# Steps 16 to 44 of a fused attention and gated feed-forward kernel: maxima and exponentials at the scheduler's highest rank

## The chip, the cores and the metric

The kernel runs on one core of a Trainium2 chip. The metric is the device time of one execution in microseconds; the runs of the kernel before took 446.5 us in the median of three (445.61 to 447.54). TensorE (PE) multiplies matrices, VectorE (DVE), ScalarE (ACT) and GpSimd (POOL) do the rest, SyncE (SP) issues most loads. Each engine works through its own row of instructions in order, and waits on semaphores where it needs another engine's result.

## What is computed

Attention with a local window and a few global keys, then a feed-forward layer with a short convolution as its gate. Cut to what matters:

```python
scores = scale * q @ k.T + bias        # bias: -slope[h] * distance
scores = where(is_global | is_local, scores, -1e9)
a = exp(scores - max(scores)); a = a / (sum(a) + 1e-9)
x = heads_joined(a @ v)                # 4 x 768 x 512
h = relu(x @ w_in)                     # 512 -> 1024
conv = conv3_over_positions(h, conv_w)
out = (h * sigmoid(conv)) @ w_out      # 1024 -> 512
```

There are 4 batches, 8 heads of width 64, 768 positions, a window of 96 keys and 8 global keys.

## The kernel before

The work is cut into 32 **jobs**: a batch, a half of its positions (384) and a pair of heads. A job has three **steps** of 128 query rows, so there are 96 steps, numbered through. Four jobs (12 steps) make one half of a batch, after which the feed-forward layer of that half can run.

One step runs through five stages. `scores` (lines 376 to 404) multiplies queries with the 232 keys in reach for both heads into a PSUM tile `s` (two buffers; up to job 8 the second head's half stands in a tile `sb` of its own). `maxima` (line 412) adds the table of distances and takes the row's minimum of the negated scores on DVE. `exps` (line 426) takes the exponentials on ACT and writes them to one of three buffers `pbuf`; where a job starts a new batch it also clears a few columns on GpSimd (line 424). `normalise` (lines 437 to 444) takes the reciprocal of the sums on DVE and scales the rows on GpSimd (and, up to step 31, on ACT). `transposes` (line 452, PE) and `evict` (line 457, ACT) bring the rows into the form `pt` that `values` (line 473, PE) multiplies with `v` into `pv`. `pv` has one PSUM bank; it is free for the next job when `mixed_high` (line 485, ACT) and `mixed_low` (line 489, DVE) have split it into `xh` and `xl`. In a name like `s41`, `mm39`, `pt38` the number is the step; in `pv12`, `xl11`, `kk14` it is the job.

The feed-forward layer uses the same splits: `h` (line 507) is the first product in three parts (`xh` with the high weights, `xl` with them, `xh` with the low weights), lines 555 to 559 are the convolution into `c`, line 577 its hyperbolic tangent, line 610 the gating, lines 612 and 613 the split into `gh` and `gl`, line 622 the second product `o`. Lines 316 to 331 decode the weights from their 64-bit words; lines 137 to 142 split queries and keys into `qh`, `ql` and `kk`.

Steps 0 to 15 are written in an order by hand. From step 16 on, the loop only states the work, and a scheduler lays out each engine's row when the kernel is built: of what its own reckoning holds ready, it takes first what has the higher rank, and rank falls in the order in which the program states the work. `values` already states its work at the highest rank. `tc.issue_after` puts some pieces behind a step's last maximum or exponential. No row can change while the kernel runs.

Of the kernel before, what the change touches and what calls it, by code (L numbers as in the profile page):

```python
# [34 lines left out]
LAG_T, LAG_V = 2, 4  # L35
NPB = 3
SHARED = 32
CHECK_EVERY = 3
HAND = 16
NATIVE = 9  # L40
# [27 lines left out]
def fast_path(tc, io):  # L68
# [273 lines left out]
    def check_piece(k):  # L342
        x = words[k]
        junk = p2.tile([P, HW], F32, tag="qh", name=f"junk{k}")
        j2 = p2.tile([P, HW], F32, tag="ql", name=f"junkb{k}")
        V.tensor_tensor_reduce(
            out=junk, in0=x, in1=x, scale=-1.0, scalar=-3.0e38,
            op0=ALU.mult, op1=ALU.max, accum_out=chk[:, k : k + 1],
        )
        A.activation(j2, x, AF.Square, accum_out=chk[:, NCHK + k : NCHK + k + 1])  # L350
        if len(words) < NCHK:
            check_load()
# [51 lines left out]
    def maxima(s):  # L404
        m, i = steps[s]
        b, u, hp = jobs[m]
        sp, c0, n, first = st_s[s]
        mm = p1.tile([P, 8], F32, tag="mm", name=f"mm{s}", bufs=6)
        for j in range(2):
            h = 2 * hp + j  # L410
            tb = tab[:, h, WIN:] if first else tab[:, h, 0:WIN]
            last_ttr[s] = V.tensor_tensor_reduce(  # L412
                out=sp[j][:, c0 : c0 + n], in0=sp[j][:, c0 : c0 + n], in1=tb,
                scale=-0.125, scalar=3.0e38, op0=ALU.add, op1=ALU.min,
                accum_out=mm[:, j : j + 1],
            )
        st_s[s] = (sp, c0, n, mm)

    def exps(s):
        m, i = steps[s]  # L420
        sp, c0, n, mm = st_s[s]
        pb = pbuf[s % NPB]
        if c0 and s and steps[s][0] % (2 * NPAIR) == 0:
            G.memset(pb[:, :, 0:c0], 0.0)
        for j in range(2):
            last_exp[s] = A.activation(  # L426
                pb[:, j, c0 : c0 + n], sp[j][:, c0 : c0 + n], AF.Exp,
                bias=mm[:, j : j + 1], scale=-1.0, accum_out=mm[:, 2 + j : 3 + j],
            )
        st_s[s] = (pb, c0, n, mm)  # L430
        if s < SHARED:
            A.activation(mm[:, 4:6], mm[:, 2:4], AF.Identity, bias=eps)

    def normalise(s):
        pb, c0, n, mm = st_s[s]
        if s >= SHARED:
            V.tensor_scalar(mm[:, 4:6], mm[:, 2:4], 1.0e-9, None, ALU.add)
        V.reciprocal(mm[:, 6:8], mm[:, 4:6])  # L438
        for j in range(2):
            x, inv = pb[:, j, c0 : c0 + n], mm[:, 6 + j : 7 + j]  # L440
            if j and s < SHARED:
                A.activation(x, x, AF.Copy, scale=inv)  # L442
# [268 lines left out]
    def check_some(cost):  # L711
        pace[0] += cost
        while pace[1] < NCHK and pace[0] >= CHECK_EVERY * (pace[1] + 1):
            check_piece(pace[1])
# [70 lines left out]
    for s in range(len(steps) + LAG_V + 1):  # L785
# [36 lines left out]
        else:  # L822
# [3 lines left out]
                manual.__exit__(None, None, None)  # L826
            if s < len(steps):
                scores(s)
                maxima(s)
                exps(s)  # L830
            k = 0
            e = s - LAG_V - 1
            if e >= 0:
# [181 lines left out]
def build(nc, io):  # L1015
    with tile.TileContext(nc, schedule_with_timeline_sim=True) as tc:
        fast_path(tc, io)
# [49 lines left out]
```

## Time and profile before

| | before |
|---|---|
| median of three runs | 446.5 us (445.61 to 447.54) |
| the profiled execution | 445.31 us |
| its span | 443.5 us |
| granted clock of PE, mean | 0.996 |
| PE busy | 431.2 us, 97% |
| DVE busy | 357.2 us, 81% |
| ACT busy | 309.9 us, 70% |
| POOL busy | 221.2 us, 50% |

The span runs from the first instruction to the last, and 1.8 us lie around it. Busy times overlap, so they don't add up. Matmuls are pipelined: one of 512 columns shows some 400 ns, while the next starts after about 234 ns, so PE counts as busy where one follows the other without a gap. A row's own work is therefore taken from start to start.

### The profile page before, as it was taken

How to read it: one execution, taken by the hardware profiler on the slowest of the kernel's cores; microseconds unless marked ns; L12 is line 12 of the kernel's file. 1: busy time of each engine (PE TensorE's matmuls, PEld its weight loads, DVE VectorE, ACT ScalarE, POOL GpSimd, SP SyncE). 2: the span in 40 equal slices, each digit the busy share in tenths (PEclk: the TensorE clock that was granted, in tenths of full speed). 3: DMA queues.
4: the chain of work that ended last, by engine and by line, in shares of the span. 5: the costliest groups of instructions: out<-in, count | busy, mean ns of one | idle time of the engine just before them, and what ended most of it. 6: DMA issues, size and time to landing. Idle time of an engine off the chain costs nothing.

```text
span 443.5 us, 9050 instructions
## 1 busy us (share of the span) xinstructions
PE 431.2 (97%) x3039; PEld 374.5 (84%) x3039; DVE 357.2 (81%) x935; ACT 309.9 (70%) x839; POOL 221.2 (50%) x307
## 2 busy tenths in 40 slices
PE   8988999799999999999999999999999999999996
PEld 7655778799889988899889988899988998798876
DVE  6899899998999988757998989747999975568700
ACT  4889988789896678546876865665776776755540
POOL 5555334654456786556757744647656841013000
PEclk9999999899999999999999999999999999999999
DMA  6998953141543244442246134423235313980111
GB/s 210 294 255 258 271 184 110 40 163 65 153 128 120 75 136 132 128 125 94 85 128 192 41 107 145 141 102 104 67 119 181 103 48 122 312 295 32 47 49 55
DMA packets 22662, 60.02 MB, mean 135 GB/s; under 512 B 3024, under 2 KB 5584, under 8 KB 22608
## 3 DMA queue, kind: packets, MB, share of 16 engines
q1 hardware_dynamic: 18992, 53.01, 39.2%
q10 hardware_dynamic: 3616, 6.36, 3.9%
q8 instruction: 26, 0.43, 0.4%
q14 instruction: 28, 0.23, 0.2%
HBM read 53.07 MB, written 6.29 MB: 134 GB/s over the span
## 4 chain that ended last, share of the span: by engine, by line
PE 81%; DVE 8%; DMA 6%; ACT 3%; issue 1%; POOL 0%; SPq 0%; DVEq 0%; ACTq 0%
PE o L622 26%; PE h L507 25%; PE pv L473 10%; PE t L452 9%; PE s L395 7%; DMA check<-in_w 3%; PE s L385 1%; PE last L643 1%; DMA out<-ob 1%; DVE w L320 1%; DVE w L318 1%; ACT junkb L350 1%; ACT pbuf L426 1%; DMA rq<-in_qk 1%; PE sb L385 1%
## 5 line engine op out<-in xcount | busy, mean ns | idle before, releaser
L444 POOL TENSOR_SCALAR pbuf<-pbuf,mm 128x232 f32<-128x232 f32 (+1 forms) x160 | 113.3, 718 | 81.0 <-DVE mm L438 49.5
L426 ACT ACTIVATE pbuf<-s,mm 128x232 f32<-128x232 f32 (+1 forms) x165 | 72.1, 442 | 48.3 <-DVE mm L412 34.6
L412 DVE CUSTOM_DVE_ANT_0 s<-s,tab 128x232 f32<-128x232 f32 (+1 forms) x165 | 63.1, 385 | 20.2 <-PE s L395 15.7
L622 PE MATMUL o<-woh,gh 128*128 128x512 f32 x184 | 74.1, 403 | 0.0
L622 PE MATMUL o<-woh,gl 128*128 128x512 f32 x184 | 73.5, 400 | 0.0
L622 PE MATMUL o<-wol,gh 128*128 128x512 f32 x184 | 73.3, 398 | 0.0
L452 PE MATMUL t<-ident,pbuf 128*128 128x128 f32 x384 | 65.4, 279 | 5.4 <-ACT pbuf L442 2.7
L557 POOL TENSOR_SCALAR c<-hbuf,cw 128x382 f32<-128x382 f32 (+1 forms) x48 | 38.6, 807 | 56.5 <-ACT hbuf L517 56.5
L452 PEld LDWEIGHTS t<-ident,pbuf 128*128 128x128 f32 x384 | 46.4, 141 | 20.2 <-ACT pbuf L442 6.4
L457 ACT ACTIVATE pt<-t 128x512 f32<-128x512 f32 x96 | 57.0, 597 | 8.3 <-PE t L452 8.0
L507 PE MATMUL h<-xl,wih 128*128 128x384 f32 x252 | 59.4, 343 | 0.0
L507 PE MATMUL h<-xh,wih 128*128 128x384 f32 x252 | 58.8, 347 | 0.1
L507 PE MATMUL h<-xh,wil 128*128 128x384 f32 x252 | 55.8, 339 | 0.0
L473 PE MATMUL pv<-pt,v 128*64 128x128 f32 (+1 forms) x768 | 50.3, 280 | 0.3 <-DVE xl L489 0.2
L473 PEld LDWEIGHTS pv<-pt,v 128*64 128x64 f32 (+1 forms) x768 | 42.5, 138 | 8.6 <-issue 3.6
L558 DVE SCALAR_TENSOR_TENSOR c<-hbuf,cw,c 128x382 f32<-128x382 f32 (+1 forms) x64 | 44.3, 699 | 4.8 <-POOL c L557 3.7
L559 DVE SCALAR_TENSOR_TENSOR c<-hbuf,cw,c 128x382 f32<-128x382 f32 (+1 forms) x64 | 45.4, 712 | 0.3
L507 PEld LDWEIGHTS h<-xh,wih 128*128 128x128 f32 x252 | 43.2, 190 | 2.1 <-ACT pbuf L426 0.9
L507 PEld LDWEIGHTS h<-xl,wih 128*128 128x128 f32 x252 | 43.9, 189 | 0.7 <-issue 0.7
L507 PEld LDWEIGHTS h<-xh,wil 128*128 128x128 f32 x252 | 44.1, 188 | 0.0
L517 ACT ACTIVATE hbuf<-h 128x384 f32<-128x384 f32 x64 | 31.4, 495 | 13.5 <-PE h L507 12.5
L622 PEld LDWEIGHTS o<-woh,gl 128*128 128x128 f32 x184 | 34.6, 188 | 7.3
(120 smaller groups left out, 856.1 us busy)
## 6 DMA issues: line engine op xcount, KB each, us to landing
v<-in_vv SPq DMA_DIRECT2D x32, 384.0 KB, 3.6
rq<-in_qk SPq DMA_DIRECT2D x23, 384.0 KB, 3.1
wr<-in_w SPq DMA_DIRECT2D x16, 512.0 KB, 5.3
check<-in_w SPq DMA_DIRECT2D x16, 512.0 KB, 4.9
rk<-in_qk SPq DMA_DIRECT2D x12, 504.0 KB, 3.6
out<-ob ACTq DMA_DIRECT2D x23, 256.0 KB, 2.4
rk<-in_qk SPq DMA_DIRECT2D x11, 408.0 KB, 3.6
rq<-in_qk SPq DMA_DIRECT2D x16, 96.0 KB, 5.1
```

The costliest lines, as they stand in the source:

```text
L412: last_ttr[s] = V.tensor_tensor_reduce(out=sp[j][:, c0 : c0 + n], in0=sp[j][:, c0 : c0 + n], in1=tb, scale=-0.125, scalar=3.0e38, op0=ALU. ...
L426: last_exp[s] = A.activation(pb[:, j, c0 : c0 + n], sp[j][:, c0 : c0 + n], AF.Exp, bias=mm[:, j : j + 1], scale=-1.0, accum_out=mm[:, 2 + ...
L444: G.tensor_scalar(x, x, inv, 1.0, ALU.mult, ALU.mult)
L452: T.transpose(pt[:, j, c, :], pb[:, j, c * P : (c + 1) * P], ident)
L457: last_ev[s] = A.activation(sb, st_pt[s], AF.Copy)
L473: T.matmul(pv[m][64 * j : 64 * j + 64, i * P : (i + 1) * P], vt[m][:n, i, c, 64 * j : 64 * j + 64], sb[:n, j, c, :], start=c == 0, stop=c ...
L507: T.matmul(ps[:, :TB], w_[:, k, fs], x_, start=part == 0 and k == 0, stop=part == 2 and k == NK - 1,)
L517: A.activation(half, ps[:, :TB], AF.Relu, scale=0.5)
L557: G.tensor_scalar(c, *tap(1), 1.0, ALU.mult, ALU.mult)
L558: V.scalar_tensor_tensor(c, *tap(0), c, ALU.mult, ALU.add)
L559: V.scalar_tensor_tensor(c, *tap(2), c, ALU.mult, ALU.add)
L622: last = T.matmul(ps, g_[:, f], w_[:, f], start=f == 0 and part == 0, stop=f == NF - 1 and part == 2,)
```

## The change

In the part that the scheduler lays out, `maxima` and `exps` of steps 16 to 44 are stated at the highest rank; a constant `FIRST` holds the first step that isn't. That covers, for each step, two maxima on DVE with their two read-outs, two exponentials on ACT, up to step 31 one addition to the sums on ACT, and twice the clearing of columns on GpSimd. The instructions stay the same; only their order in the rows, and with it the order of all that the scheduler lays out around them, differs, from 61.5 us on in the trace of before to some 236 us.

```diff
--- before.py
+++ after.py
@@ -35,6 +35,7 @@
 LAG_T, LAG_V = 2, 4
 NPB = 3
 SHARED = 32
+FIRST = 45
 CHECK_EVERY = 3
 HAND = 16
 NATIVE = 9
@@ -826,8 +827,11 @@
                 manual.__exit__(None, None, None)
             if s < len(steps):
                 scores(s)
-                maxima(s)
-                exps(s)
+                with contextlib.ExitStack() as es:
+                    if s < FIRST:
+                        es.enter_context(tc.high_priority())
+                    maxima(s)
+                    exps(s)
             k = 0
             e = s - LAG_V - 1
             if e >= 0:
```

What that does to the rows is shown at three places. The numbers behind the underscore are the build's own; lines of the changed kernel are one higher than before.

PE, at the scores of step 22 (`s22` one head, `sb22` the other), before:

```order
L385 MATMUL s22_1070<-rk7_794,rq7_795 128x232
L473 MATMUL pv5_1026<-pt17_957,v5_800 64x128 x4
L473 MATMUL pv5_1026<-pt15_854,v5_800 64x128 x4
L473 MATMUL pv5_1026<-pt16_915,v5_800 64x128 x4
L452 MATMUL t19_1042<-ident_153,pbuf1_194 128x128 x2
L385 MATMUL sb22_1071<-rk7_794,rq7_795 128x232
```

and with the change:

```order
L386 MATMUL s22_1070<-rk7_794,rq7_795 128x232
L386 MATMUL sb22_1071<-rk7_794,rq7_795 128x232
L474 MATMUL pv5_1026<-pt17_957,v5_800 64x128 x4
L474 MATMUL pv5_1026<-pt15_854,v5_800 64x128 x4
L474 MATMUL pv5_1026<-pt16_915,v5_800 64x128 x4
L453 MATMUL t19_1042<-ident_153,pbuf1_194 128x128 x4
```

The second head's scores moved ahead of the values of job 5.

DVE, up to the split `xl6` of job 6, before:

```order
L141 TENSOR_TENSOR kk10_1335<-rk10_1253,kk10_1335 64x816
L320 SCALAR_TENSOR_TENSOR w7_0_1250<-wr7_0_1010,w7_0_1250 128x512
L558 SCALAR_TENSOR_TENSOR c0_865<-hbuf_190,cw_185,c0_865 128x382
L412 ISA s27_1285,mm27_1290<-s27_1285,tab_166 128x136
L412 ISA mm27_1290 128x1
L438 RECIPROCAL mm26_1261<-mm26_1261 128x2
L316 TENSOR_SCALAR w7_1_1329<-wr7_1_1065 128x512
L331 TENSOR_TENSOR wol_189<-w6_1_1199,woh_188 128x512
L412 ISA s28_1342,mm28_1347<-s28_1342,tab_166 128x232
L412 ISA mm28_1347 128x1
L489 TENSOR_TENSOR xl6_1222<-pv6_1171,xh6_1221 128x384
```

and with the change:

```order
L317 TENSOR_SCALAR w7_1_1329<-wr7_1_1065 128x512
L332 TENSOR_TENSOR wol_189<-w6_1_1199,woh_188 128x512
L413 ISA s28_1342,mm28_1347<-s28_1342,tab_166 128x232
L413 ISA mm28_1347 128x1
L319 SCALAR_TENSOR_TENSOR w7_1_1329<-wr7_1_1065,w7_1_1329 128x512
L559 SCALAR_TENSOR_TENSOR c0_865<-hbuf_190,cw_185,c0_865 128x382
L142 TENSOR_TENSOR kk10_1335<-rk10_1253,kk10_1335 64x816
L413 ISA s28_1342,mm28_1347<-s28_1342,tab_166 128x232
L413 ISA mm28_1347 128x1
L490 TENSOR_TENSOR xl6_1222<-pv6_1171,xh6_1221 128x384
L439 RECIPROCAL mm26_1261<-mm26_1261 128x2
```

The second maximum of step 27 stands next to the first, `kk10` went behind it, and `w7_1` of line 318 (319 now) and the second maximum of step 28 came ahead of `xl6`.

PE, at the values of job 7, which need `xl6` done, before:

```order
L452 MATMUL t24_1270<-ident_153,pbuf0_193 128x128 x4
L395 MATMUL s29_1399<-kk9_1204,qh9_1202 128x232
L395 MATMUL s29_1399<-kk9_1204,ql9_1203 128x232
L395 MATMUL s29_1399<-kk9_1204,qh9_1202 128x232
L395 MATMUL s29_1399<-kk9_1204,ql9_1203 128x232
L473 MATMUL pv7_1299<-pt23_1233,v7_1068 64x128 x4
L473 MATMUL pv7_1299<-pt21_1133,v7_1068 64x128 x4
L473 MATMUL pv7_1299<-pt22_1192,v7_1068 64x128 x4
```

and with the change:

```order
L453 MATMUL t24_1270<-ident_153,pbuf0_193 128x128 x4
L474 MATMUL pv7_1299<-pt23_1233,v7_1068 64x128 x4
L474 MATMUL pv7_1299<-pt21_1133,v7_1068 64x128 x4
L474 MATMUL pv7_1299<-pt22_1192,v7_1068 64x128 x4
L396 MATMUL s29_1399<-kk9_1204,qh9_1202 128x232
L396 MATMUL s29_1399<-kk9_1204,ql9_1203 128x232
L396 MATMUL s29_1399<-kk9_1204,qh9_1202 128x232
L396 MATMUL s29_1399<-kk9_1204,ql9_1203 128x232
```

The scores of step 29 went from ahead of the values to behind them.

DVE, at the split `xl11` of job 11, before:

```order
L412 ISA s39_1903,mm39_1908<-s39_1903,tab_166 128x232
L412 ISA mm39_1908 128x1
L489 TENSOR_TENSOR xl11_1974<-pv11_1917,xh11_1973 128x384
L613 TENSOR_TENSOR gl0_2_1577<-hbuf_190,gh0_2_1576 128x8x2
L438 RECIPROCAL mm38_1874<-mm38_1874 128x2
L141 TENSOR_TENSOR kk14_1956<-rk14_1865,kk14_1956 64x1008
L412 ISA s39_1903,mm39_1908<-s39_1903,tab_166 128x232
L412 ISA mm39_1908 128x1
L610 SCALAR_TENSOR_TENSOR hbuf_190<-c1_1541,hbuf_190 128x8x128
L613 TENSOR_TENSOR gl0_3_1851<-hbuf_190,gh0_3_1850 128x1024
L412 ISA s40_1963,mm40_1968<-s40_1963,tab_166 128x232
L412 ISA mm40_1968 128x1
```

and with the change (the rows further up are `gl0_2`, `gl0_3`, a maximum of step 39, a gating and `gl0_4`, which before stood behind `xl11`):

```order
L614 TENSOR_TENSOR gl0_4_1947<-hbuf_190,gh0_4_1946 128x1024
L142 TENSOR_TENSOR kk14_1956<-rk14_1865,kk14_1956 64x1008
L438 TENSOR_SCALAR mm39_1908<-mm39_1908 128x2
L413 ISA s40_1963,mm40_1968<-s40_1963,tab_166 128x232
L413 ISA mm40_1968 128x1
L614 TENSOR_TENSOR gl0_5_2001<-hbuf_190,gh0_5_2000 128x1024
L413 ISA s41_2018,mm41_2023<-s41_2018,tab_166 128x232
L413 ISA mm41_2023 128x1
L490 TENSOR_TENSOR xl11_1974<-pv11_1917,xh11_1973 128x384
L439 RECIPROCAL mm39_1908<-mm39_1908 128x2
L413 ISA s40_1963,mm40_1968<-s40_1963,tab_166 128x232
L413 ISA mm40_1968 128x1
```

`xl11` moved behind eleven instructions that followed it before.

PE, at the values of job 12, which need `xl11` done, before:

```order
L507 MATMUL h2_2_2062<-xl11_1974,wih_186 128x384
L507 MATMUL h2_2_2062<-xh8_1521,wil_187 128x384
L507 MATMUL h2_2_2062<-xh9_1677,wil_187 128x384
L507 MATMUL h2_2_2062<-xh10_1832,wil_187 128x384
L507 MATMUL h2_2_2062<-xh11_1973,wil_187 128x384
L473 MATMUL pv12_2094<-pt38_1992,v12_1820 64x128 x4
L473 MATMUL pv12_2094<-pt36_1894,v12_1820 64x128 x4
L473 MATMUL pv12_2094<-pt37_1938,v12_1820 64x128 x4
L395 MATMUL s42_2067<-kk14_1956,qh14_1954 128x232
```

and with the change:

```order
L508 MATMUL h2_2_2062<-xh11_1973,wih_186 128x384
L508 MATMUL h2_2_2062<-xl8_1522,wih_186 128x384
L508 MATMUL h2_2_2062<-xl9_1678,wih_186 128x384
L508 MATMUL h2_2_2062<-xl10_1833,wih_186 128x384
L474 MATMUL pv12_2094<-pt38_1992,v12_1820 64x128 x4
L474 MATMUL pv12_2094<-pt36_1894,v12_1820 64x128 x4
L474 MATMUL pv12_2094<-pt37_1938,v12_1820 64x128 x4
L508 MATMUL h2_0_2005<-xl11_1974,wih_186 128x384
L508 MATMUL h2_0_2005<-xh8_1521,wil_187 128x384
L508 MATMUL h2_0_2005<-xh9_1677,wil_187 128x384
L508 MATMUL h2_0_2005<-xh10_1832,wil_187 128x384
```

The third part of `h2_0`, `h2_1` and `h2_2` (with `wil`) and their product with `xl11`, 15 matmuls, moved from ahead of the values to behind them.

## Rows read from the trace of the kernel before

**Rows 1.** The page, part 1: engine, busy us (share of the span), weight loads and others behind it.

```profile
PE 431.2 (97%) x3039; PEld 374.5 (84%) x3039; DVE 357.2 (81%) x935; ACT 309.9 (70%) x839; POOL 221.2 (50%) x307
```

**Rows 2.** Busy time by stage: stretch, its us, busy us of each engine, PEclk, DMA share, GB/s.

```profile
80.00:120.00 40.00, 37.70 (x287) 34.84 (x287) 38.03 (x91) 34.03 (x92) 19.05 (x23) 0.96 0.35 108
...
120.00:160.00 40.00, 40.00 (x288) 36.21 (x287) 39.01 (x92) 30.95 (x81) 27.63 (x31) 1.00 0.33 101
```

**Rows 3.** PE in order of time: start, us, line, form, count [idle before, released by].

```profile
39.41 0.44 PE L452 MATMUL t<-ident,pbuf 128*128 128x128 f32 x2 [1.04 <-DMA rq<-in_qk]
...
81.49 0.60 PE L452 MATMUL t<-ident,pbuf 128*128 128x128 f32 x4
...
84.15 0.38 PE L395 MATMUL s<-kk,qh 128*128 128x232 f32 x1 [2.06 <-ACT pbuf L426]
...
85.10 2.61 PE L473 MATMUL pv<-pt,v 128*64 128x128 f32 x24 [0.24 <-DVE xl L489]
...
87.64 1.11 PE L452 MATMUL t<-ident,pbuf 128*128 128x128 f32 x4
...
92.20 1.54 PE L473 MATMUL pv<-pt,v 128*64 128x128 f32 x24
```

**Rows 4.** Busy time by stage, with the granted clock, around three places of rows 3.

```profile
39.40:41.40 2.00, 1.99 (x24) 1.53 (x26) 1.97 (x8) 1.80 (x7) 1.38 (x2) 1.00 0.72 194
...
84.00:86.00 2.00, 1.61 (x15) 1.43 (x16) 2.00 (x5) 2.00 (x8) 1.36 (x2) 0.84 0.04 15
...
86.00:88.00 2.00, 2.00 (x19) 1.67 (x17) 2.00 (x6) 0.70 (x2) 0.00 (x0) 0.50 0.00 0
```

**Rows 5.** DVE in order of time, 60 to 85 us.

```profile
60.26 0.69 DVE L318 SCALAR_TENSOR_TENSOR w<-wr,w 128x512 int32<-128x512 int32 x1
...
60.87 0.61 DVE L558 SCALAR_TENSOR_TENSOR c<-hbuf,cw,c 128x382 f32<-128x382 f32 x1
...
64.04 0.41 DVE L412 CUSTOM_DVE_ANT_0 sb<-sb,tab 128x232 f32<-128x232 f32 x1 [0.75 <-PE sb L385]
...
66.14 1.20 DVE L558 SCALAR_TENSOR_TENSOR c<-hbuf,cw,c 128x382 f32<-128x382 f32 x1
...
84.49 0.55 DVE L489 TENSOR_TENSOR xl<-pv,xh 128x384 fp32r<-128x384 f32 x1
```

**Rows 6.** Waits: engine, line, releaser: us in total, times, longest; DVE 62 to 146 us, PE whole span.

```profile
DVE s L412 <- PE s L395: 1.3, 1, 1.3
...
DVE sb L412 <- PE sb L385: 0.7, 1, 0.7
...
PE t L452 <- DMA rq<-in_qk: 1.0, 1, 1.0
```

**Rows 7.** GpSimd in order of time.

```profile
66.11 0.83 POOL L138 CAST qh<-rq 128x768 fp32r<-128x768 f32 x1
```

**Rows 8.** The chain of work that ended last, in order of time: start, us, what.

```profile
96.55 0.44 PE s L395 x4
...
96.99 0.44 PE t L452 x4
...
97.43 3.30 PE h L507 x19
```

**Rows 9.** DVE in order of time, 132 to 143 us.

```profile
132.51 0.39 DVE L412 CUSTOM_DVE_ANT_0 s<-s,tab 128x232 f32<-128x232 f32 x1
...
132.83 0.55 DVE L489 TENSOR_TENSOR xl<-pv,xh 128x384 fp32r<-128x384 f32 x1
...
142.25 0.16 DVE L437 TENSOR_SCALAR mm<-mm 128x2 f32<-128x2 f32 x1
...
142.44 0.17 DVE L438 RECIPROCAL mm<-mm 128x2 f32<-128x2 f32 x1
...
142.53 1.05 DVE L142 TENSOR_TENSOR ql<-rq,qh 128x768 fp32r<-128x768 f32 x1
```

**Rows 10.** PE in order of time, values of job 12.

```profile
139.72 1.54 PE L473 MATMUL pv<-pt,v 128*64 128x128 f32 x24
```

## The prediction, made before the changed kernel had run

> **What bounds the kernel now.** I read the page's busy times first [rows 1]: TensorE (PE) is busy 97% of the span, VectorE (DVE) 81%. A busy PE is not a PE at its peak, so the second view was the busy time by stage [rows 2]: of the two stages from 80 to 160 us PE is covered in one and lacks 2.30 us in the other, and DVE is nearly as full (38.03 and 39.01 of 40 us). Work that only moves can therefore gain no more than PE loses now; what it can lose has no such bound. The third view, PE in order of time [rows 3], shows the loss in the steps that the change touches. It is one place. PE has issued its transposes at 81.49 and is done with them at 82.09; the next scores start at 84.15, after 2.06 us of idle time, and the next values (`pv`, 24 records) at 85.10, after 0.24 us more, released by DVE's `xl`. Then those values take 2.61 us where the same 24 take 1.54 later, and four transposes 1.11 where they took 0.60: the granted clock is 0.84 and 0.50 in the two stretches from 84 to 88 us [rows 4], so it fell to the lower level, 1.2 GHz, after PE had idled. The place costs 2.30 us of waiting and some 1.8 us of slow clock (1.07 and 0.51 from those rows, about 0.2 on the matmuls between, by estimate), 4.1 us in all. An idle time of 1.04 us ahead of 39.41 [rows 3] left the clock at 1.00 [rows 4].
>
> **What the wait hangs on.** `pv` of job 7 needs the one PSUM bank of `pv`, which is free when DVE has done `xl` of job 6. DVE did that from 84.49 to 85.04 [rows 5], and from 62 to 146 us it waited for PE only twice, 0.7 and 1.3 us [rows 6]. So DVE's place in its own row sets the time here, not what it waits for.
>
> **The change, part by part.** It adds and removes no instruction; it gives a rank, and the scheduler's order follows. Nothing differs ahead of 61.5 us. Three places decide. An instruction's cost on an engine that never stops is the time from its start to the next one's.
>
> *Place 0, steps 22 and 23.* The second half of step 22's scores now stands ahead of `pv` of job 5 (first pair of order rows). DVE's maxima of that half waited 0.75 us for it at 64.04 [rows 5]. PE has 1.5 us of values between the two positions [rows 3], so that wait goes: DVE runs 0.75 us earlier from there. PE itself only swaps equal work: nothing.
>
> *Place 1, `xl` of job 6 and `pv` of job 7.* Ahead of `xl6` DVE now has two instructions more (a weight operation of line 318, 0.61 us from 60.26 to 60.87 [rows 5], and a maximum, 0.32 us from 132.51 to 132.83 [rows 9]) and one reciprocal less (0.09, from 142.44 to 142.53): +0.84 us, which the 0.75 us from place 0 nearly pays. `xl6` ends at 85.04 + 0.84 - 0.75 = 85.13, and `pv7` starts at about 85.2. On PE the scores of step 29 went from ahead of `pv7` to behind it: four matmuls, 0.44 us [rows 8]. PE so arrives at the same 82.09, waits 3.1 us in one piece, and has 0.44 us still to do that it had done before: 0.1 + 0.44, **+0.5 us**. The slow clock stays, as the idle time is no shorter. What would shorten it is less lengthening on DVE: the convolution's instruction at 66.14 took 1.20 us beside a GpSimd cast (66.11 to 66.94) [rows 7], one without such company 0.61 at 60.87 [rows 5].
>
> That row agrees with the Trainium skill, "SBUF — State Buffer", section "SBUF: two separate sides": a VectorE operation with two SBUF inputs and a GpSimd operation that reads SBUF share one pair of ports as an exclusive lock, so that the later one blocks. By that rule, which casts fall beside which DVE instructions moves the sum of place 1 by one such blocking, 0.6 us either way by this row; the order alone doesn't tell which, and the sum above takes the same lengthening as before.
>
> *Place 2, `xl` of job 11 and `pv` of job 12.* Here both engines move apart. On PE, 15 matmuls of `h` that stood ahead of `pv12` stand behind it now: 15 x 0.174 = 2.61 us (19 took 3.30 [rows 8]), so PE, if nothing held it, would reach `pv12` at 139.72 [rows 10] - 2.61 = 137.1. On DVE, `xl11` ran at 132.83 [rows 9]. Now eleven instructions of the gate split, the maxima and `kk` that followed it stand ahead; behind it, up to `ql` of job 15, are only a reciprocal and two maxima (0.09 + 2 x 0.32 = 0.73 us). The work up to that `ql` is the same set but for two tiny ones that went behind it (0.28 us, from 142.25). `ql` starts at 142.53 before; so with DVE's idle time as it was, `xl11` would end at 142.53 - 0.28 - 0.73 = 141.5. With all of DVE's waits for PE gone, 0.75 and 1.3 us [rows 5, 6], it ends at 139.4; I put the early end half a microsecond lower still, at 138.9, for one blocking less. I take the 0.75 us of place 0 and half of the 1.3 (PE's scores of step 32 come somewhat earlier): 140.1.
>
> `pv12` then starts 140.1 - 137.1 = **3.0 us** late against the same work before; with the two ends, 1.8 to 4.4. This contains place 1's 0.5 us, since DVE, not PE, sets it. Part of it shows earlier: the scores of step 41 stand 18 matmuls of `h` and six transposes earlier on PE (18 x 0.174 + 6 x 0.11 = 3.8 us [rows 8]), and wait for the exponentials of step 39, which wait for DVE too.
>
> *The rest.* On ScalarE the evictions `pt` slide behind exponentials; around place 2 what they wait for is done before `xl11`. SP's queue swaps loads of `v` with `rq` and `rk` a place or two; PE's only wait for a load is the one at 39.41 [rows 3, 6], so I cost it at nothing, and at about that 1 us if its cover is gone. The order is the same again from 236 us, and with PE at 97% no later slack gives the time back.
>
> **The sum.** The profiled execution took 445.31 us (span 443.5 and 1.8 around it), 1.2 us under the median of 446.5. On that execution it is 445.3 + 3.0 = 448.3; carried to the median, 446.5 + 3.0 = **449.5 us**.
>
> **The rivals.**
> *The waits are hidden*: DVE gets ahead further than its own waits tell, because casts and two-input instructions meet less often; `xl11` by 138.5, and 0.5 to 1.4 us are lost: about 447.5. For it: the row at 66.14, 0.6 us longer than its like, and it isn't the only one. Against it: DVE's row up to `ql` of job 15 holds the same work as before, and GpSimd's does too.
> *The old stall goes*: if `xl6` comes 2 us earlier, PE waits for 1 us there, which left the clock at 1.00 before [rows 3, 4], and the place gives back 2.0 + 1.8 - 0.44 = 3.4 us; if place 2 then loses 1 us or nothing, 443.1 to 444.1. Against it: +0.84 us of work ahead of `xl6`.
> *The clock falls again* (the far side): the 3 us of place 2 are split over up to three waits (scores of step 41, `xh11`, `pv12`). An idle time of 1.04 us left the clock alone, 2.30 us in two pieces did not; these lie between. If it falls there as it fell at 85 us, 1.8 us more: 451.3. It decides if the wait at `pv12` comes out like that one, not in thirds.
> That the rank lifts nothing is excluded by the order, but it doesn't lift evenly: the maxima of steps 29 and 30 stand later on DVE than before.
>
> **How the numbers follow.** Forecast, +1.8 to +4.4: 0.43. Clock falls: 0.12. Hidden: 0.28. Stall goes: 0.17. Half a per cent, 2.2 us, is about what a measurement of this kernel can tell from no change. Slower by more than that: 0.43 + 0.12 = 0.55 (the little of the forecast below 2.2 us is set against the clock's upper end); within: 0.28; faster: 0.17. The range goes from 444.2, which leaves out most of the faster case, to 452.8, past the clock's case. The forecast's own range is 448.3 to 450.9.
>
> **What would show it.** Right: DVE's 0.75 us wait at the scores of step 22 is gone; PE idles about 3 us ahead of `pv` at 82 to 85 us, and the stretches behind it show half the clock; between 133 and 141 us PE waits, last for DVE's `xl`, longest 1 to 3 us; the same work on PE comes 2 to 4 us later from there. Wrong: no idle PE at 133 to 141 us (hidden), a full clock from 84 to 88 us (stall gone), or a clock below 1 after 133 us (the slow side). It would also be wrong if PE waited for a `t` or `s` at some place after 142 us where I found none.

## The result: 1.2% slower, and where the time went

| | before | with the change |
|---|---|---|
| median | 446.17 us (444.99 to 447.54, 6 runs) | 450.71 us (450.33 to 453.18, 6 runs) |
| ratio | | 1.0116 (1.0090 to 1.0143) |
| the profiled execution, its span | 445.31, 443.5 | 450.62, 448.8 |

The changed kernel is slower by 4.5 us in the medians and by 5.3 us in the profiled executions; the forecast said 3.0. The sign was right and the time lies inside the forecast's own range of 448.3 to 450.9 us, but both losses are above the 4.4 us that the forecast had as its upper end: six runs put the median of before at 446.17, three had put it at 446.5. The page, part 1, answers to [rows 1]:

```profile
PE 432.2 (96%) x3039; PEld 374.7 (83%) x3039; DVE 360.5 (80%) x935; ACT 309.1 (69%) x839; POOL 222.4 (50%) x307
```

The same instructions ran. PE is busy 1.0 us longer, so some 4.3 of the 5.3 us are idle time of PE. Which waits these are stands in PE's row in order of time (start, us, line, form, count, in brackets the idle time before and what ended it), beside [rows 3 and 10]:

```profile
61.53 1.54 PE L474 MATMUL pv<-pt,v 128*64 128x128 f32 x24
...
68.35 0.66 PE L386 MATMUL s<-rk,rq 64*128 64x232 f32 x2 [0.99 <-ACT pbuf L427]
...
82.59 0.62 PE L508 MATMUL h<-xh,wih 128*128 128x384 f32 x2 [0.72 <-ACT xh L486]
83.05 0.60 PE L453 MATMUL t<-ident,pbuf 128*128 128x128 f32 x4
86.31 2.83 PE L474 MATMUL pv<-pt,v 128*64 128x128 f32 x24 [2.67 <-DVE xl L490]
...
130.19 0.44 PE L453 MATMUL t<-ident,pbuf 128*128 128x128 f32 x2 [0.37 <-DVE mm L438]
...
136.91 0.37 PE L396 MATMUL s<-kk,qh 128*128 128x232 f32 x1 [0.36 <-ACT pbuf L427]
...
139.74 0.44 PE L453 MATMUL t<-ident,pbuf 128*128 128x128 f32 x2 [0.95 <-POOL pbuf L445]
...
142.42 1.54 PE L474 MATMUL pv<-pt,v 128*64 128x128 f32 x24 [0.16 <-issue]
```

The first row is `pv5`, the one at 86.31 `pv7`, the last `pv12`. Place 0 has a new wait of 0.99 us, place 1 waits of 0.72 and 2.67 where there were 2.06 and 0.24, and place 2 four short ones. `pv12` starts 80.89 us after `pv5`, before 78.21; the 2.61 us of `h` that went behind it count on top, so PE is 80.89 - 78.21 + 2.61 = 5.3 us late there. That is the whole difference of the spans: from `pv12` to the end it takes 306.4 us now and took 303.8 + 2.61 = 306.4 before, so nothing of it comes back.

The short waits tell less than they cost. In this view a transpose pair of 0.38 us is followed after 0.14 us when nothing holds PE, so each idle time behind one begins some 0.24 us after PE could have gone on.

The stages (stretch, its us, busy us and count of PE, PEld, DVE, ACT and POOL, granted clock, DMA share, GB/s) answer to [rows 2 and 4]:

```profile
80.00:120.00 40.00, 36.61 (x259) 34.12 (x259) 37.35 (x88) 33.31 (x92) 17.79 (x23) 0.91 0.30 96
120.00:160.00 40.00, 38.16 (x288) 33.50 (x287) 36.70 (x90) 31.62 (x84) 29.66 (x33) 1.00 0.38 119
...
86.00:88.00 2.00, 1.69 (x16) 1.69 (x18) 2.00 (x5) 1.64 (x7) 1.58 (x2) 0.50 0.71 209
88.00:90.00 2.00, 2.00 (x16) 1.67 (x13) 1.69 (x3) 2.00 (x7) 0.30 (x2) 0.50 0.05 9
90.00:92.00 2.00, 2.00 (x11) 2.00 (x10) 1.88 (x4) 1.91 (x8) 0.20 (x1) 0.50 0.94 321
```

Behind the wait at place 1 the clock falls to its lower level, 1.2 GHz, as it did before. It stays there until 92 us; before, it was back at the upper level within the stretch from 88 to 90 us (mean 0.81). Behind place 2 it stays at 1.00. From 120 to 160 us PE lacks 1.84 us, where before it lacked none.

DVE's row is what the forecast rested on (`xl6` at 85.70, `xl11` at 141.78; beside [rows 5 and 9]). First two rows of before:

```profile
64.37 0.73 DVE L331 TENSOR_TENSOR wol<-w,woh 128x512 fp32r<-128x512 f32 x1
...
68.18 0.68 DVE L318 SCALAR_TENSOR_TENSOR w<-wr,w 128x512 int32<-128x512 int32 x1
```

and with the change:

```profile
62.62 0.40 DVE L413 CUSTOM_DVE_ANT_0 sb<-sb,tab 128x232 f32<-128x232 f32 x1
...
63.27 1.10 DVE L332 TENSOR_TENSOR wol<-w,woh 128x512 fp32r<-128x512 f32 x1
...
64.82 1.34 DVE L319 SCALAR_TENSOR_TENSOR w<-wr,w 128x512 int32<-128x512 int32 x1
...
85.70 0.55 DVE L490 TENSOR_TENSOR xl<-pv,xh 128x384 fp32r<-128x384 f32 x1
...
141.78 0.55 DVE L490 TENSOR_TENSOR xl<-pv,xh 128x384 fp32r<-128x384 f32 x1
142.25 0.15 DVE L439 RECIPROCAL mm<-mm 128x2 f32<-128x2 f32 x1
```

DVE no longer waits for the scores of step 22. But the two weight operations behind it take 1.10 and 1.34 us, where the like took 0.73 and 0.68 before, and `xl6` ends at 85.70 + 0.55 = 86.25 instead of the 85.13 of the forecast. Its waits from 62 to 142 us (line, releaser: us, times, longest), beside [rows 6]:

```profile
DVE gl L614 <- ACT gh L613: 1.1, 1, 1.1
DVE c L611 <- ACT sat L589: 0.6, 1, 0.6
DVE c L559 <- ACT c L556: 0.3, 1, 0.3
```

The waits for PE (0.7 and 1.3 us) are gone, as forecast. Three waits for ScalarE came in their place, 2.0 us together. `xl11` is done when the next instruction starts, at 142.25, not 140.1.

GpSimd in order of time, at place 0 (beside [rows 7]) and at place 2:

```profile
64.35 1.28 POOL L138 CAST kk<-rk 128x816 fp32r<-128x816 f32 x1 [0.52 <-PE sb L386]
65.58 1.28 POOL L139 CAST qh<-rq 128x768 fp32r<-128x768 f32 x1
...
135.97 3.71 POOL L445 TENSOR_SCALAR pbuf<-pbuf,mm 128x232 f32<-128x232 f32 x2 [0.39 <-PE s L396]
```

Both casts of job 9 now run beside DVE's long instructions from 64.82 to 67.2 us, and take 1.28 us each, where the second took 0.83.

### The profile page after: what moved, and what is told of

It reads as the page before. It is cut to its first block, busy times and chain, and to the rows that moved or that the text cites. A ratio compares the mean times of both kernels' runs of the same rounds, so it can differ in the third digit from the quotient of the medians.

```text
span 448.8 us, 9061 instructions
## 1 busy us (share of the span) xinstructions
PE 432.2 (96%) x3039; PEld 374.7 (83%) x3039; DVE 360.5 (80%) x935; ACT 309.1 (69%) x839; POOL 222.4 (50%) x307
## 4 chain that ended last, share of the span: by engine, by line
PE 67%; DVE 17%; DMA 6%; ACT 6%; issue 2%; POOL 1%; SPq 0%; DVEq 0%; ACTq 0%; POOLq 0%
PE o L623 24%; PE h L508 20%; PE pv L474 7%; PE t L453 7%; PE s L396 5%; DMA check<-in_w 5%; DVE s L413 2%; DVE c L559 2%; DVE c L560 2%; ACT pbuf L427 2%; DVE gl L614 2%; DVE kk L142 1%; PE s L386 1%; PE last L644 1%; DVE hbuf L611 1%
## 5 line engine op out<-in xcount | busy, mean ns | idle before, releaser
L445 POOL TENSOR_SCALAR pbuf<-pbuf,mm 128x232 f32<-128x232 f32 (+1 forms) x160 | 114.8, 728 | 95.1 <-DVE mm L439 55.2
L453 PE MATMUL t<-ident,pbuf 128*128 128x128 f32 x384 | 66.7, 282 | 6.7 <-ACT pbuf L443 2.7
L558 POOL TENSOR_SCALAR c<-hbuf,cw 128x382 f32<-128x382 f32 (+1 forms) x48 | 37.5, 785 | 59.4 <-ACT hbuf L518 59.4
L508 PE MATMUL h<-xh,wih 128*128 128x384 f32 x252 | 60.3, 348 | 1.0 <-ACT xh L486 0.7
L623 PEld LDWEIGHTS o<-woh,gh 128*128 128x128 f32 x184 | 34.8, 189 | 7.2 <-issue 0.7
```

What stands on the lines that cost most here:

```text
L445: G.tensor_scalar(x, x, inv, 1.0, ALU.mult, ALU.mult)
L453: T.transpose(pt[:, j, c, :], pb[:, j, c * P : (c + 1) * P], ident)
L508: T.matmul(ps[:, :TB], w_[:, k, fs], x_, start=part == 0 and k == 0, stop=part == 2 and k == NK - 1,)
L558: G.tensor_scalar(c, *tap(1), 1.0, ALU.mult, ALU.mult)
L623: last = T.matmul(ps, g_[:, f], w_[:, f], start=f == 0 and part == 0, stop=f == NF - 1 and part == 2,)
```

## The experiments

**The theories.** *PE's waits*: what PE loses at each place is what counts, so taking away the long wait at place 1, or the slow clock behind it, gives 2 us or more back. *DVE's row*: it sets the pace up to place 2, so that a wait of PE ahead of it costs nothing of its own, and only what makes DVE earlier helps. A third question is what makes DVE late. (The expectations, written one batch after the other, put these in their own words.)

**Rows laid by hand.** A rank moves many instructions at once. To move single ones, the part from step 16 on was taken out of the scheduler's hands: the program notes its instructions there instead of issuing them, and then issues them in a listed order.

```diff
+    rows = Rows(); V, A, G, T, Y = map(rows.engine, (nc.vector, nc.scalar, nc.gpsimd, nc.tensor, nc.sync))
...
+                rows.on = True
...
+    rows.play(ORDER)
```

With the order of either kernel in the list, each engine's row is that kernel's but for a few instructions on PE and ACT where the listed part begins. In these kernels all lines are those of the changed kernel, also where the order is that of before. `rows_before` and `rows_after` test the instrument. `rows_first` has the order of after through places 0 and 1 and that of before from there on; `rows_second` the other way round.

> Every engine's row from step 16 on is laid down by hand in the order that the kernel before has; nothing else differs. It only shows whether rows laid by hand keep the time. Both theories: within 0.3% of the kernel before, some 446 us, with the same wait of 2.1 us ahead of the scores at 84 us.

> The same with the rows of the changed kernel. Both theories: 1.009 to 1.014 times the kernel before, some 451 us, with TensorE's waits of 1.0 us at 68, 0.7 and 2.7 us at 82 to 86, and 1.8 us in all from 130 to 143 us.

> The changed kernel's rows up to 117 us, the rows of before from there on: places 0 and 1 alone. Theory of the trace after: 1.0 us at the scores of step 24 and 2.2 us more at the values of job 7 (2.9 instead of 2.3 us of waiting, and a longer stretch at the lower clock), so 3.2 us, some 449.4 us. Theory of the prediction: place 0 gains nothing and costs nothing on TensorE, place 1 costs 0.5 us, so some 446.7 us.

> The rows of before up to 117 us, the changed kernel's from there on: place 2 alone. Theory of the trace after: 2.5 us, some 448.7 us, lost at the transposes of steps 36 to 38, which wait for GpSimd's scaling; the values of job 12 wait less than 0.5 us for the split of job 11. Theory of the prediction: 2.5 to 3.0 us, lost at the values of job 12 and in the steps ahead of them, last for DVE's split of job 11, 1 to 3 us in one piece.

The start of `pv5` itself lies anywhere from 61.1 to 64.0 us in these executions, whatever the kernel, so places are counted from it. (Where it lies at 62.5 us or later, the clock had already stood at 0.50 for a stretch between 24 and 44 us; where it lies below 62 us, it had not.) From `pv12` to the end of the span it takes 306.1 to 306.8 us in every kernel that has the order of after there, so the place of `pv12` decides. The last two columns are read from PE and DVE in order of time.

| kernel | median us | ratio to before (95%) | `xl11` on DVE, us after `pv5` | `pv12` on PE, us after `pv5` |
|---|---|---|---|---|
| before | 446.61 | | 71.32 | 78.21 |
| rows_before | 444.86 | 0.9971 (0.9949 to 0.9994) | 70.94 | 77.83 |
| rows_after | 451.41 | 1.0111 (1.0083 to 1.0139) | 80.32 | 80.97 |
| rows_first | 448.37 | 1.0045 (1.0021 to 1.0070) | 73.88 | 80.94 |
| rows_second | 448.80 | 1.0057 (1.0038 to 1.0077) | 77.99 | 78.64 |

`before` ran again in every batch, and each ratio is to the `before` of its own: 446.61 us here, 446.37 for `xl6_up`, `xl6_recip_up`, `clock_filler` and `no_cast_reads`, 445.71 for the other four.

`rows_before` came out 0.3% faster than before, 0.4 us of it seen in the trace, so the others are held against it. With `h` counted as above, `pv12` is 80.97 - 77.83 + 2.61 = 5.75 us late in `rows_after` and 78.64 - 77.83 + 2.61 = 3.4 in `rows_second`; in `rows_first`, where `h` stands as before, it is 80.94 - 77.83 = 3.1 us late, near the 3.2 expected from the trace after and not the 0.5 of the prediction. (`xl11` has another place in DVE's row in `rows_after` and `rows_second`, so it is compared between these two only, and between the other two.) Places 0 and 1 cost some 3 us alone, and so does place 2; together they cost less than the sum. PE of `rows_second`, in order of time:

```profile
85.20 0.38 PE L396 MATMUL s<-kk,qh 128*128 128x232 f32 x1 [2.07 <-ACT pbuf L427]
86.15 1.54 PE L474 MATMUL pv<-pt,v 128*64 128x128 f32 x24 [0.24 <-DVE xl L490]
...
128.99 0.44 PE L453 MATMUL t<-ident,pbuf 128*128 128x128 f32 x2 [0.84 <-DVE mm L438]
...
135.70 0.38 PE L396 MATMUL s<-kk,qh 128*128 128x232 f32 x1 [0.35 <-ACT pbuf L427]
...
138.53 0.44 PE L453 MATMUL t<-ident,pbuf 128*128 128x128 f32 x2 [0.94 <-POOL pbuf L445]
...
141.21 1.54 PE L474 MATMUL pv<-pt,v 128*64 128x128 f32 x24 [0.16 <-issue]
```

The last three waits are those of the changed kernel, to within 0.01 us, although PE had not lost the 3 us of places 0 and 1. PE and DVE arrive 2.33 us sooner than in `rows_after`, and both by the same amount. That speaks for DVE's row.

**Taking PE's waits away at place 1.** Four kernels, from `rows_after`. DVE's row, names as in the order above:

```diff
+L490 xl6 <- pv6, xh6                 (xl6_up)
+L439 RECIPROCAL mm26                 (xl6_recip_up, sums_up)
 L413 s28, first maximum
 L319 w7_1
 L559 c0
 L142 kk10
 L413 s28, second maximum
-L490 xl6 <- pv6, xh6
-L439 RECIPROCAL mm26                 (xl6_recip_up, sums_up)
```

`sums_up` also moves the reciprocal of step 27 ahead of `w7_1`, `c0`, `ql10` and a product of the weights (line 332), and that of step 28 ahead of `ql11` and two gatings. `clock_filler` leaves the rows as they are and puts 22 multiplications of `ident` with itself on PE ahead of `pv7`, into the tile of step 25's transposes, which is overwritten after; they keep PE busy through the wait.

> The changed kernel's rows laid by hand, and on DVE the split xl6 stands ahead of the maxima of step 28 instead of behind six more instructions: it can then run at 82.7 us instead of 85.7, so the values of job 7 start at 83.5 instead of 86.3. Theory that xl6 alone holds place 1: the wait of 2.7 us and the lower clock behind it go, 5 to 5.9 us, so 445.5 to 446.5 us against 451.4 of the rows of after. Rival, which I hold: a second wait stands right behind. ScalarE's exponentials of step 27 queue behind its scaling of step 26, which needs DVE's reciprocal of step 26, still at 86.2 us; so the scores of step 29 wait until 87.2 us, about 2 us in one piece at the end of the values, and only some 2 us are gained, 449 us.

> The same with the reciprocal of step 26 moved up as well, right behind xl6. By the rival of the run before, both waits go: TensorE idles less than 1 us from 80 to 92 us at full clock, 5 to 5.9 us are gained against the rows of after, 445.5 to 446.5 us. By the theory that xl6 alone counts, it is no better than the run before.

> The changed kernel's rows laid by hand, and on TensorE 22 extra multiplications of the identity with itself ahead of the values of job 7 (their result is overwritten by the transposes of step 25), 22 x 0.11 = 2.4 us of the 2.7 us that it waits there. Theory that idling lowers the clock and the lower clock costs about 3 us behind it (0.9, 1.1 and 1.0 us above the usual in the three stretches from 86 to 92 us): the clock stays at 1.00 and some 3 us are gained, 448.4 us. Rival: the clock falls anyway, or what comes faster then waits for DVE: within 0.5 us of the rows of after, 451.4 us.

> The rows of xl6_recip_up, and on DVE the reciprocals of steps 27 and 28 stand as early as their sums are there: ahead of the last weight operation of job half 7 and of the split of the queries, and ahead of two gating operations (they stood 3.0 and 4.7 us later, at 89.1 and 96.8 us). Theory that a chain of reciprocals on DVE, with ScalarE's scalings and splits queued behind them, holds TensorE from 82 to 98 us, wait after wait: the waits of 3.3 and 1.6 us at 90 and 98 us go, the values of job 9 start 42.5 to 43.5 us after those of job 5 (45.6 to 45.8 in the rows of after and in all three edits of place 1), and 2 to 3 us are gained against the rows of after, some 448.5 us. Rival, that DVE's work as a whole is the bound up to 98 us, in whatever order: 45.6 us again, within 0.7 us of 451.4.

| kernel | median us | ratio to before (95%) | `xl11` after `pv5` | `pv12` after `pv5` |
|---|---|---|---|---|
| xl6_up | 450.93 | 1.0103 (1.0080 to 1.0126) | 80.36 | 81.01 |
| xl6_recip_up | 450.59 | 1.0103 (1.0079 to 1.0126) | 80.30 | 80.94 |
| clock_filler | 452.66 | 1.0156 (1.0130 to 1.0182) | 80.34 | 80.99 |
| sums_up | 452.13 | 1.0133 (1.0098 to 1.0169) | 80.31 | 80.96 |

The gains expected of them, 2 us and more, did not come, and the theory of PE's waits falls. PE of `xl6_up` in order of time shows the wait move on:

```profile
84.63 1.54 PE L474 MATMUL pv<-pt,v 128*64 128x128 f32 x24
88.66 0.37 PE L396 MATMUL s<-kk,qh 128*128 128x232 f32 x1 [2.50 <-ACT pbuf L427]
...
91.80 0.44 PE L508 MATMUL h<-xh,wih 128*128 128x384 f32 x1 [1.03 <-ACT xh L486]
```

`pv7` starts without a wait, 22.05 us after `pv5` instead of 24.78, and the next scores wait 2.50 us for the exponentials, which stand on ScalarE behind the scaling of step 26, which needs that step's reciprocal. With the reciprocal moved too, the wait goes one step further, to the next `xh`, behind the scaling of step 27. PE of `xl6_recip_up`:

```profile
90.09 0.44 PE L508 MATMUL h<-xh,wih 128*128 128x384 f32 x1 [3.31 <-ACT xh L486]
...
98.46 0.44 PE L453 MATMUL t<-ident,pbuf 128*128 128x128 f32 x2 [1.57 <-POOL pbuf L445]
```

Its clock stayed up, although PE had idled longer than anywhere before (stages as above):

```profile
88.00:90.00 2.00, 0.00 (x0) 0.00 (x0) 1.74 (x4) 0.74 (x3) 0.67 (x1) 1.00 0.27 49
90.00:92.00 2.00, 1.91 (x11) 1.91 (x12) 1.89 (x7) 2.00 (x7) 0.28 (x1) 1.00 0.93 356
```

So two of the kernels settle the clock as well, for their profiled executions: in `xl6_recip_up`, and in `clock_filler` from 86 to 90 us, it was 1.00, and `pv12` did not come sooner. What PE loses at the lower clock lies inside the time that it would wait anyway. The median of `clock_filler` is 1.3 us above that of `rows_after`, though. Its profiled execution was its fastest, 450.06 us at a mean granted clock of 0.998; the other five took 452.0 to 454.2 at 0.991 to 0.996, and where their clock fell is not on record. `sums_up` frees all three reciprocals; there `pv8` is on PE where it is in `rows_before`, 0.07 us early for the same work. From 36 to 85 us behind `pv5`, DVE's row is the same as in `rows_after` within 0.07 us, and `pv12` within 0.01.

**What makes DVE late.** `no_cast_reads` replaces job 9's two casts on GpSimd at place 0 by clearing of the same tiles, which reads nothing:

```diff
-            G.tensor_copy(kk, rk)
-            G.tensor_copy(qh, rq)
+            G.memset(kk.bitcast(F32), 0.0) if m == 9 else G.tensor_copy(kk, rk)
+            G.memset(qh.bitcast(F32), 0.0) if m == 9 else G.tensor_copy(qh, rq)
```

> The changed kernel's rows laid by hand; the two casts of keys and queries of job 9 on GpSimd, at 64.4 and 65.6 us, are replaced by fills of the same tiles with zero, so GpSimd reads nothing there (the scores of job 9 lose these parts, the output is not the reference's). Theory that DVE's two-input instructions are held by GpSimd's casts: DVE's weight operation at 64.8 takes 0.68 instead of 1.34 us and the convolution's at 66.2 0.6 instead of 1.1; the maxima of step 23 come 1.1 us earlier, TensorE's wait of 1.0 us at 68 us goes, and xl6 comes some 1 us earlier too: 1.5 to 2.5 us gained, 449 to 450 us. Rival, that these instructions are long by themselves or by their place: 1.3 and 1.1 us again and 451.4 us.

DVE in order of time, first `rows_after`:

```profile
65.82 1.35 DVE L319 SCALAR_TENSOR_TENSOR w<-wr,w 128x512 int32<-128x512 int32 x1
...
67.17 1.09 DVE L559 SCALAR_TENSOR_TENSOR c<-hbuf,cw,c 128x382 f32<-128x382 f32 x1
```

and `no_cast_reads`, with the same instruction started at the same time:

```profile
64.27 1.10 DVE L332 TENSOR_TENSOR wol<-w,woh 128x512 fp32r<-128x512 f32 x1
...
65.82 0.68 DVE L319 SCALAR_TENSOR_TENSOR w<-wr,w 128x512 int32<-128x512 int32 x1
...
66.50 0.59 DVE L559 SCALAR_TENSOR_TENSOR c<-hbuf,cw,c 128x382 f32<-128x382 f32 x1
```

0.67 and 0.50 us are back; `L332`, which runs beside another cast that was left in, stays at 1.10. `xl11` came at 79.04 and `pv12` at 79.69 us behind `pv5`: each 1.28 us sooner (expected were 1.5 to 2.5), carried in full from 66 to 142 us. The median is 450.47, ratio 1.0105 (1.0075 to 1.0136): 0.9 us less than `rows_after`, and by the ratios 0.3, in the direction of the trace, but too little for the medians to prove alone. PE's 0.99 us wait of place 0 is gone there, and its 2.7 us wait for `xl6` is not.

These rows agree with the Trainium skill, "SBUF — State Buffer", section "SBUF: two separate sides", by which a VectorE instruction with two SBUF inputs and a GpSimd instruction that reads SBUF exclude each other for a whole instruction; the clearing, which reads nothing, left the two-input instructions at their short times.

**Place 2.** `xl11_up` moves `xl11` up on DVE and, as it needs it, `xh11` on ScalarE ahead of an eviction and a gate split. `xl11_up_scale_act` also takes the scalings of steps 37 and 38 from GpSimd to ScalarE.

```diff
 L614 gl0_4
+L490 xl11 <- pv11, xh11
 L142 kk14
 L438 mm39
 L413 s40
 L614 gl0_5
 L413 s41
-L490 xl11 <- pv11, xh11
...
-            if j and s < SHARED:
+            if j and s < SHARED or s in (37, 38):        (xl11_up_scale_act)
```

> The changed kernel's rows laid by hand; the split of job 11 moves up on both engines, xh11 on ScalarE ahead of an eviction and a split of the gate (136.8 instead of 138.2 us), xl11 on DVE behind the second next split of the gate: it ends at about 138.6 instead of 142.3 us. The prediction's step for place 2, that the values of job 12 are late because xl11 stands behind eleven instructions: 2 to 3 us gained, some 449 us. Rival, from the trace after: TensorE itself arrives only at 142.3 us, since it has waited for GpSimd's and ScalarE's work on steps 36 to 39; the values of job 12 start 35.1 to 35.4 us after those of job 9 as before, less than 0.4 us gained, 451 us.

> The same, and the scaling of steps 37 and 38 runs on ScalarE for both heads instead of on GpSimd, where these four took 2.3, 0.45, 2.3 and 1.4 us beside DVE's two-input operations. If the two waits stand side by side (DVE's split and GpSimd's scaling), taking both away gains 1.0 to 2 us against the rows of after, some 450 us: the values of job 12 start 33.4 to 34.4 us after those of job 9. If something third holds TensorE there: within 0.5 us of the run before.

In `xl11_up`, `xl11` came at 76.66 us behind `pv5`, 3.66 sooner than in `rows_after`, and `pv12` at 79.93, only 1.04 sooner, which lies between the two expectations (median 450.12, ratio 1.0097, 1.0064 to 1.0130). So `xl11` alone does not hold `pv12`. Where most of the 1.04 us seem to come from stands in GpSimd's row, against the 3.71 us at 135.97 of after:

```profile
135.78 2.76 POOL L445 TENSOR_SCALAR pbuf<-pbuf,mm 128x232 f32<-128x232 f32 x2 [0.38 <-DVE mm L439]
```

These are the two scalings of step 38. Together they are 0.95 us shorter here, where `xl11`, which reads PSUM, stands between the gate split and `kk14`, which read SBUF twice each. PE's 0.95 us wait for them, at 139.74 of after, is gone in `xl11_up`. With the scalings on ScalarE, `pv12` came at 80.31 and the time was 451.19 (ratio 1.0126, 1.0095 to 1.0157): PE then waits 0.73 us for exponentials that stand behind them. That is 0.38 us later than in `xl11_up`; the 1 to 2 us expected did not come. Freeing one engine there leaves the next.

**The other direction.** `needed_first` takes the order of before and puts what PE waits for at place 1 ahead of work that nobody waits for: the second maximum of step 27, the reciprocal of step 26 and `xl6` ahead of `kk10`, a weight operation and a convolution; the reciprocal of step 27 and `xl7` likewise; on ScalarE the exponentials of step 27 ahead of an eviction. The transposes of step 24 then read their buffer after the exponentials of step 27 have written it, so its values are not those of before; its instructions are.

```diff
 L413 s27, first maximum
+L413 s27, second maximum
+L439 RECIPROCAL mm26
+L490 xl6 <- pv6, xh6
 L142 kk10
 L321 w7_0
 L559 c0
-L413 s27, second maximum
-L439 RECIPROCAL mm26
...
-L490 xl6 <- pv6, xh6
```

> The rows of the kernel before laid by hand, with what TensorE waits for moved up from 80 to 90 us: on DVE the second maximum of step 27, the reciprocals of steps 26 and 27 and the splits xl6 and xl7 ahead of splits of keys, weight operations and convolutions; on ScalarE the exponentials of step 27 ahead of an eviction. Theory that the order on DVE and not its amount of work holds TensorE: the waits of 2.1 and 0.2 us at 84 us and the lower clock behind them go, at most 1 us of waiting comes back at the values of job 8 and at step 30; 2 to 3.5 us gained against the rows of before (444.9 us), some 442 us, and faster than both kernels. Rival, that DVE's work as a whole is the bound: the waits move to later places, within 0.7 us of 444.9.

It took 445.64 us, ratio 0.9993 (0.9972 to 1.0013): the 2 us and more expected of it did not come, and it lies 0.8 us behind `rows_before`. The stall and the lower clock at 84 us are gone (82 to 90 us at 1.00), and PE waits further on. PE in order of time:

```profile
89.40 0.33 PE L396 MATMUL s<-kk,qh 128*128 128x136 f32 x1 [0.82 <-ACT pbuf L427]
...
116.41 1.54 PE L474 MATMUL pv<-pt,v 128*64 128x128 f32 x24 [1.33 <-ACT pt L458]
```

`xl11` and `pv12` are both 0.75 us later than in `rows_before`. These are not of the edit: DVE is 0.93 us late already at the first maximum of step 27, ahead of all that was moved. Most of that arises at 75.70 us, where a weight operation of line 317 with one input takes 1.09 us instead of 0.42, beside a cast of keys that waited for a load and started just ahead of it, at 75.64; in `rows_before` it started just behind it. Without that the edit would have gained some 0.2 us, by estimate. Before the change, too, the 4.1 us of place 1 are not there for the taking by this edit.

## Why the prediction was right, and where not

*What bounds the kernel.* Right, and more strictly than the text said. It took DVE's row as what sets place 2. In `rows_after`, `xl6_up`, `xl6_recip_up`, `clock_filler`, `sums_up`, `rows_second` and `no_cast_reads`, `pv12` starts 0.64 or 0.65 us after `xl11` starts, wherever that lies between 77.99 and 80.36 us.

*Place 0.* DVE's 0.75 us wait is gone, as forecast; the credit of 0.75 us was lost again, as two instructions got longer, the one at 63.27 by 0.37 us and that at 64.82 by 0.66. "PE itself only swaps equal work: nothing" was wrong on two sides. The scores of both heads of step 22 now run side by side and take 0.60 us together (60.93 to 61.53), where each took 0.59 alone before, so PE saves some 0.6 us. And the scores of step 24 wait 0.99 us for exponentials; `no_cast_reads` ties that to the casts, since the wait goes with them.

*Place 1.* The term that was mis-sized: +0.5 us by the text, 3.1 by `rows_first`, which has places 0 and 1. "The sum above takes the same lengthening as before" was the choice at fault; the text had named 0.6 us either way for it, and the two instructions are longer by 1.03 us together. And `xl6` is not the end of what PE needs there: behind it stand the reciprocals of steps 26 to 28 and their scalings, as the moving waits of `xl6_up` and `xl6_recip_up` show, and of these the text said nothing. That the slow clock stays was right for this trace; by `xl6_recip_up` and `clock_filler` it adds nothing to `pv12`'s lateness, as what PE loses by it lies inside the later waits.

*Place 2.* Alone it costs 3.4 us by `rows_second`, and `xl11` ends there at 77.99 + 0.47 us behind `pv5`, which on the clock of before (61.51) is 139.97: the text had 140.1 and 3.0 us. That these agree is in part luck. The text took 1.4 us of DVE's waits off, 0.75 at place 0 and half of the 1.3 us for the scores of step 32; `rows_second` keeps the first (0.7) and lost the second wholly. Either way 1.2 of the 2.6 us are left that DVE waited from 62 to 142 us before. What the term lacked is that DVE comes to place 2 later by 80.32 - 77.99 = 2.33 us when places 0 and 1 are changed as well, of which the casts of job 9 make 1.28 and DVE's waits some 0.9 (2.1 us in `rows_after`, all for ScalarE; 1.2 in `rows_second`). In the profile of the changed kernel `xl11` is done at 142.25, 2.15 us later than the text's 140.1, and `pv12` starts 0.17 us behind it; with the text's 3.0 these make its 5.3 us, where the text's own sign was "2 to 4 us later". So "this contains place 1's 0.5 us" holds for what PE loses, not for what DVE loses.

*Which wait is last.* The text said PE would wait last for `xl`, longest 1 to 3 us. The longest wait is 0.95 us, for GpSimd's scaling; the last, 0.16 us ahead of `pv12`, ends 0.17 us after `xl11` is done. And `xl11_up` shows that `xl11` was not alone in holding `pv12`: 3.66 us sooner, it gave 1.04. DVE's row acts on place 2 not through `xl11` alone: the waits ahead of it are for exponentials and for GpSimd's scaling, which need DVE's maxima and reciprocals.

*The rivals.* "The waits are hidden" fell, as they lengthened; so did "the old stall goes", for `xl6` came later. "The clock falls again" did not happen: 1.00 from 120 to 160 us. *The rest* was right: PE's lateness of 5.3 us at `pv12` is that of the span, so what lies behind neither gave back nor took more.

**Left open.** What else holds `pv12` when `xl11` is early was not taken apart further. Nor was it tried to take every collision of DVE and GpSimd away, so it isn't known how much of DVE's pace is work and how much is blocking. No kernel here beats both; `rows_before` is the fastest, 0.3% under before with almost the same order, for which no cause is shown.

## What to carry to other kernels

When one engine waits for a second that is hardly ever idle in that stage (DVE was busy for 76.8 of the 80 us from 62 to 142 before, 77.1 after), moving what it waits for ahead may only move the wait on, as in four kernels here: follow the second engine's row to its next consumer, and count what makes that whole row earlier or later. An idle time that a reorder removes may be spent at once where two-input DVE instructions then meet GpSimd's casts, so read beside each moved DVE instruction what GpSimd does at that time. Raising the rank of what looks urgent puts other needed work later, here the reciprocals and `xl`.

## What the runs showed of the hardware that was not expected

The length of an idle time of PE alone does not tell whether the clock falls behind it. Idle times of 2.06 us (before) and 2.67 us (after) had 0.50 behind them; 2.07 us in `rows_second`, 2.50 in `xl6_up` and 3.31 in `xl6_recip_up` were followed by 1.00. (In `rows_second` and `xl6_up` the clock had been at 0.50 before, at some 40 to 43 us; in `xl6_recip_up` it had not.) `rows_second` in stages shows it behind the same wait as before:

```profile
84.00:86.00 2.00, 0.71 (x4) 0.52 (x4) 2.00 (x8) 1.67 (x7) 1.55 (x2) 1.00 0.47 173
86.00:88.00 2.00, 1.85 (x27) 1.68 (x28) 2.00 (x4) 1.77 (x5) 0.86 (x1) 1.00 0.00 0
```

These are single profiled executions, and no run here shows the cause.

Of the four GpSimd scalings of 128x232 at place 2 of the changed kernel, one took 0.45 us and the others 2.29, 2.33 and 1.40; beside these three DVE's instructions with two SBUF inputs (1.0 to 1.3 us each) stood one behind the other, beside the short one DVE's maxima. And the 22 filler multiplications showed as 44 records over 5.08 us, two records and 0.23 us for each multiplication, twice the 0.11 us of a transpose from which they had been sized, so `pv7` came 2.2 us later there than in the changed kernel, and `pv12` still did not move.
